# Gated linear attention and feed-forward block: block sums on VectorE, paired stores, an earlier load and later bias copies

## The chip, the cores and the metric

The kernel runs on one core of one Trainium2 chip. The metric is the time of one execution in microseconds (us); the time of a kernel is the median of its runs. Profiles come from one execution that the hardware profiler recorded, and their instants count from the first instruction of that execution.

## What is computed

```python
x  = A_x                                   # 1 x 2048 x 576, fp32
xn = layernorm(x)
q, k, v = split(xn @ wqkv)                 # 32 heads of 18
pq, pk = phi(q), phi(k)                    # phi(t) = (t + 1 if t > 0 else exp(t)) + 1e-6
kv = sum_s pk[s] (outer) v[s]              # no mask: one state per head for the whole sequence
z  = sum_s pk[s]
o  = (pq @ kv) / (pq . z + 1e-6)
s  = o @ wo
h  = gelu(xn @ w1 + b1)                    # 576 x 4608
g  = silu(h @ w2 + b2)                     # 4608 x 576
out = x + s * g
```

Everything is fp32. The kernel writes each operand of a matmul as a high part (a cast to the fp32r format of TensorE) and a low part (what the cast left), and multiplies high by high, high by low and low by high. The large products are also written as seven products of half-size blocks instead of eight, which is why sums and differences of blocks are needed as operands beside the blocks themselves.

## The kernel before

**Three phases.** Phase 1 (to about 152 us) normalises x, makes its operands, and computes keys, values and the state. Phase 2 (about 152 to 312 us) computes the queries and the attention output. Phase 3 (from about 312 us) is the feed-forward block with its gate. The rows of x are handled as eight pairs of row tiles in phases 1 and 2, and as two halves in phase 3.

**Rounds of phase 2.** The loop over `r` (line 1094 and after) has one round for a pair of tiles; `base = (NPAIR + r) * NSP`, with 14 steps to a round. In rounds 1 to 7 TensorE runs the seven products of `Proj` (steps 0 to 6, in the order 1, 6, 7, 5, 2, 4, 3; lines 382 to 408), which make the queries, and from round 2 two `Attend` (28 matmuls each, in steps 7 to 12), which multiply the weighted queries of two rounds earlier by the folded output weights. After each `Attend` come five transposes for the round before (`transpose_p`). Each product of `Proj` is emptied out of its PSUM bank by VectorE or ScalarE: product 6 at line 393, product 7 at line 396, products 5, 4 and 3 at line 386, the first half of a query at line 402. The bank of product 7 is used again by product 4, and that of product 5 by product 3, so these two wait for the emptying.

**The order is written out by hand.** `add(step, function)` puts a call on a list, and `at_step(step)` runs the list of that step behind the product of that step. All of phases 1 and 2 is inside `in_order()`, which fixes the order of every engine and of the DMA queue of SyncE (SP) to that of the program text: an instruction that waits holds everything behind it on its engine. In phase 3 the order of TensorE, VectorE, ScalarE and GpSimd is fixed in the same way; that of SP is not.

**Rest.** D is 576 = 4 x 128 + 64, so each half of the inner dimension is 2 x 128 + 32 rows. The last 32 rows of x and of w1 do not fill a pass of TensorE. `Rest` (line 912) therefore stacks the high part of four things of 32 rows with their low parts, so that one pass does all of their products. One `Rest` handles one such stack: seven of them are made, `RESTS` names them (two of x, five of w1), and the `Rest` number r is loaded in round r and worked on in round r + 1. Its steps are

- the load of 128 x 512 fp32 raw rows into a tile of the pool `stg` (line 917; six buffers, shared with the raw wo rows, the folded weights and the attention outputs),
- `hi(0)` on ScalarE and `lo(0)` on VectorE for three blocks, as they are (lines 923 and 927),
- `store(0)`: four DMAs on SP, one for each group of 32 rows, because the stack holds each of the two parts twice (line 934),
- `sums` on GpSimd: four subtractions or additions of 128 x 128 blocks, in place (lines 940 and 942),
- `hi(1)`, `lo(1)`, `store(1)` for the four sums.

`hi` takes a buffer of the pool `w1r` under the tag `stw`, of which there are two. From round 3 on, the sums of w2 blocks (`w2_hi`, `w2_lo`, lines 533 to 540) take the same two buffers, twice in a round, at steps 9 and 11, and give them back when their store has landed.

**The fold.** Round 0 multiplies the state into wo (`fold_wo`, line 847) and moves the result by three rows of SP copies (lines 858 and 861) into other partitions. `wo` is loaded ahead of it at line 816. The raw rows of the first `Rest` are loaded behind it, at step 9 of round 0.

**Phase 3** runs 18 blocks of 28 steps, nine to a half of the rows: 14 steps of `Up` (two groups of seven products of seven matmuls) and 14 of the products with w2, which add into `macc`. `macc` begins as a copy of the bias b2: `set_bias` (line 1254, ScalarE), four copies of 128 x 1152, at steps 2, 3, 5 and 6 of the first block of half 0 and at steps 12, 13, 15 and 17 of the first block of half 1. The bias itself is loaded, spread over all partitions, by `load_bias` (line 1247) into a buffer under the tag `w2t6`. The same buffer is taken next by `load_sum(7)` (line 1329, at step 5), into which `sum7` (line 520, a DMA of GpSimd's queue that adds, at step 16) adds another block. `W2_SUMS_FIRST` gives the steps at which three ready operands of w2 are loaded back in the first block.

Of the kernel before, what the change touches and what calls it, by code (L numbers as in the profile page):

```python
# [8 lines left out]
F32 = mybir.dt.float32  # L9
# [6 lines left out]
P = 128  # L16
# [10 lines left out]
RW = 32  # L27
# [11 lines left out]
NPAIR = NT // 2  # L39
# [6 lines left out]
def linear_attention_gated_ffn(ctx, tc, x, wqkv, wo, w1, w1e, b1, w2, b2, out):  # L46
    nc = tc.nc
# [77 lines left out]
    xe_dram = [dram.tile([P, 4, 7, P], F32, name=f"xe_dram{i}") for i in range(2)]  # L125
    we_dram = [dram.tile([P, 4, 7, P], F32, name=f"we_dram{i}") for i in range(NB4)]
# [19 lines left out]
    class Weight:  # L146
# [28 lines left out]
        def sums(self, raw, eng):  # L175
            r4 = raw.rearrange("p (k f d) -> p k f d", k=4, f=2)
            f0a, f0b, f1a, f1b = r4[:, 0:2, 0], r4[:, 2:4, 0], r4[:, 0:2, 1], r4[:, 2:4, 1]
            self.t = [
                stage_w1(f"wt{i}")[:, : 2 * D].rearrange("p (i k d) -> p i k d", i=2, k=2)
                for i in range(2)  # L180
            ]
            a, b = self.t
            T = {4: a[:, 0], 5: a[:, 1], 6: b[:, 0], 7: b[:, 1]}
            for i, u, v in ((5, f1a, f0a), (6, f1b, T[5]), (7, f1b, f1a), (4, f0b, T[6])):
                eng.tensor_tensor(T[i], u, v, op=SUB)
# [358 lines left out]
    def add(step, fn, *args):  # L544
        plans.setdefault(step, []).append((fn, args))
# [105 lines left out]
    def plan_pair(p):  # L651
# [19 lines left out]
        add(base + 3, do_state, p - 1)  # L671
        if p == 1:
            sums(1, (0, 0, 0, 1, 1), 1, 6, GP)
            add(base, phi_max, k_ts[0][1], e_t[1])
            add(base, phi_add, k_ts[0][1])
# [11 lines left out]
            add(base + 5, x_rest, 2, 1)  # L687
            add(base + 5, x_lo, 2, 1)
            sums(2, (6, 6, 6, 6, 7), 8, 9, GP)
            add(base + 5, x_lo_tmp, 2)  # L690
            add(base + 6, wkq.sums_hi, 1)
# [8 lines left out]
        else:  # L700
# [6 lines left out]
            if p + 1 < NPAIR:  # L707
                q = p + 1
                add(base, x_norm, q, 1)
                add(base + 3, transpose_x, q, 1)  # L710
                add(base + 3, x_hi, q, 1)
                add(base + 3, x_rest, q, 1)
                sums(q, (4, 4, 4, 6, 5), 7, 10, DV)
                add(base + 4, x_lo, q, 1)
                add(base + 6, x_lo_tmp, q)
# [39 lines left out]
    for p in range(1, NPAIR):  # L755
        plan_pair(p)
        base = p * NSP
# [22 lines left out]
    def q_tiles(r):  # L780
        return [r_bufs[(2 * r + s) % 4] for s in range(2)]
# [11 lines left out]
    base = NPAIR * NSP  # L793
# [118 lines left out]
    class Rest:  # L912
# [15 lines left out]

        def store(self, g):
            t, at = self.t, slice(3 * g, (3, 7)[g])  # L930
            for j in range(4):
                v = t[:, j % 2 if self.of_x else j // 2].bitcast(F32)
                dst = (xe_dram if self.of_x else we_dram)[self.i][RW * j : RW * (j + 1)]
                nc.sync.dma_start(dst.rearrange("r c i j -> (r c) i j")[:, at], v)

        def sums(self):
            a, b, c, d = (self.s[:, k] for k in range(4))
            tt = nc.gpsimd.tensor_tensor
            if self.of_x:
                tt(d, a, d, op=SUB), tt(c, c, d, op=SUB), tt(a, c, a, op=ADD), tt(b, b, c, op=SUB)  # L940
            else:
                tt(a, d, a, op=SUB), tt(d, c, d, op=SUB), tt(c, c, a, op=SUB), tt(b, b, c, op=SUB)
# [125 lines left out]
                    t, self.ops[i] = op_tile(w1p, [W1_K[i], P], tag, bufs, f"w{i}_{n}")  # L1068
                nc.sync.dma_start(t.bitcast(F32), w1_dram[n % NP, i])

    rests, kept = {}, []
    RESTS = ((0, True), (0, False), (1, False), (2, False), (3, False), (4, False), (1, True))
    X_OVER = {1: (xSH, 8, 0), 2: (xH, 7, 1), 4: (xH, 4, 2)}
    X_EXTRA = (5, 3, 6, 7)
# [15 lines left out]
    for r in range(NPAIR + 2):  # L1090
        base = (NPAIR + r) * NSP
# [3 lines left out]
        if r < NPAIR:  # L1095
            a, b = q_tiles(r)
# [15 lines left out]
        if 1 <= r < NPAIR:  # L1112
            a, b = q_tiles(r)
            at = base + 2 * (r == 2)
# [12 lines left out]
        if 3 <= r <= 7:  # L1127
            n = 2 * r + 3
            for j in range(2):
                add(base + (4, 5)[j], w2_sum, n + j, True)  # L1130
                add(base + (9, 11)[j], w2_hi, n + j)
                add(base + (10, 11)[j], w2_lo, n + j)
        if r < NPAIR - 1:
            i, of_x = RESTS[r]
            add(base + (1 if r else 9), lambda r=r, i=i, of_x=of_x: rests.update({r: Rest(i, of_x)}))
        if 1 <= r < NPAIR:
            at = base + (5 if r == 1 else 1)
            for g, k in ((0, 0), (1, 4)):
                add(at + k, lambda r=r, g=g: rests[r - 1].hi(g))
                add(at + k, lambda r=r, g=g: rests[r - 1].lo(g))  # L1140
                add(at + k + 2, lambda r=r, g=g: rests[r - 1].store(g))
            add(at + 2, lambda r=r: rests[r - 1].sums())
        if r == NPAIR - 1:
            add(base + 8, load_x_over, 0)
        if r == 0:
# [18 lines left out]
        if 1 <= r < NPAIR:  # L1164
            for s in range(2):
                at = Attend(r - 2, s) if r >= 2 else None
# [14 lines left out]
        elif r == NPAIR:  # L1181
            w = w1t[0]
            at = Attend(r - 2, 0)
# [6 lines left out]
            at = Attend(r - 2, 1)  # L1190
# [12 lines left out]
        elif r > NPAIR:  # L1203
            for s in range(2):
                at = Attend(r - 2, s)
# [27 lines left out]
    kept = None  # L1233
# [7 lines left out]
    C11, C12, C21, C22, U1 = range(5)  # L1241
# [341 lines left out]
    PW2 = {1: 3, 7: 4, 3: 6}  # L1583
    PW2_FIRST = {1: 3, 2: 4, 7: 8, 3: 9}
    W2_SUMS_NEXT = {5: 23, 6: 27}
    W2_SUMS_FIRST = {4: 4, 5: 6, 6: 10}
    W2_NEXT = {1: 15, 2: 17, 7: 19, 4: 21, 5: 23, 3: 25, 6: 27}
    PH = dict(
        S={(7, 0): 7, (5, 0): 8, (6, 0): 10, (3, 0): 11, (7, 1): 13, (5, 1): 14, (6, 1): 15, (3, 1): 15},
# [19 lines left out]
    for step in range(n_chunks):  # L1609
        half, c = divmod(step, NC)  # L1610
        base = step * NS
        plain = step == n_chunks - 1
        h = HOps(c)
        if c == 0:
            if half:
                add(base + 2, load_bias)
            for at, m in zip((12, 13, 15, 17) if half else (2, 3, 5, 6), (C11, C22, C21, C12)):
                add(base + at, set_bias, m)
        if half == 0:
            plan_w1(add, w1t[2 * step + 1], base, **P1)  # L1620
# [7 lines left out]
            if step == 0:  # L1628
                for i, at in W2_SUMS_FIRST.items():
                    add(at, w2t[0].load, i)  # L1630
# [79 lines left out]
        for j in range(CF // 2):  # L1710
            n = 2 * step + j
# [54 lines left out]
```

## Time and profile before

| | us |
|---|---|
| median of 3 runs | 1143.37 (1142.31 to 1144.32) |
| the profiled execution | 1141.5 |
| its span, first to last instruction | 1139.7 |
| TensorE / VectorE / ScalarE / GpSimd busy | 1102.4 / 808.2 / 515.4 / 464.4 |
| first query product of round 3 | at 200.17 |
| end of the rounds (the last two attention tiles begin) | at 294.86 |
| moved by DMA | 295.0 MB, 259 GB/s on average |

The span lies 1.8 us below the time of the same execution and 3.7 us below the median. Busy time of TensorE is modelled for overlapping matmuls, so it says when the engine had work, not that it worked at its peak. "PEclk" in the views is the granted clock of TensorE as a share of full speed, and "DMA share" is the mean busy share of the 16 DMA engines.

### The profile page before, as it was taken

The page shows a single profiled execution, that of the slowest core. Times are in us where ns is not written, and L with a number is a line of the kernel's source. Part 1 is how long each engine was busy: PE and PEld are TensorE (multiplying, and loading weights), DVE is VectorE, ACT ScalarE, POOL GpSimd, SP SyncE. Part 2 cuts the span into 40 slices and gives each one's busy share as a digit, 9 for nine tenths or more (in the row PEclk, how much of TensorE's full clock was granted, in tenths as well). Part 3 has the DMA queues.
Part 4 walks back from the last instruction along what each step waited for, and adds up shares of the span by engine and source line. Part 5 has one row for each costly group of instructions (what it writes and reads, how often), then busy time and mean ns, then how long its engine had stood idle before and what let it go on. Part 6 is the DMA issues. An engine that isn't in the chain of part 4 may idle for free.

```text
span 1139.7 us, 19018 instructions
## 1 busy us (share of the span) xinstructions
PE 1102.4 (97%) x6888; PEld 1015.4 (89%) x6888; DVE 808.2 (71%) x1260; ACT 515.4 (45%) x945; POOL 464.4 (41%) x445
## 2 busy tenths in 40 slices
PE   8999996888979999999999999999999999999998
PEld 8999996888969889899899898998998988989988
DVE  6777476657558888888888898684674764755776
ACT  7776454444454454444435445543242242342342
POOL 6853524554524525525445344133232242341310
PEclk9999998999989999999999999999999999999999
DMA  5987838997797887967968969998766667767343
GB/s 199 322 282 261 276 90 267 346 352 289 289 368 223 311 280 243 349 223 259 347 209 288 320 190 328 384 390 292 231 218 230 219 213 227 223 223 234 92 151 114
DMA packets 116219, 295.02 MB, mean 259 GB/s; under 512 B 12637, under 2 KB 31581, under 8 KB 114079
## 3 DMA queue, kind: packets, MB, share of 16 engines
q1 hardware_dynamic: 110655, 282.61, 70.4%
q0 software_dynamic: 4896, 10.03, 5.2%
q8 instruction: 54, 0.88, 0.3%
q10 hardware_dynamic: 576, 1.18, 0.3%
q14 instruction: 38, 0.31, 0.1%
HBM read 180.39 MB, written 108.66 MB: 254 GB/s over the span
## 4 chain that ended last, share of the span: by engine, by line
PE 81%; DVE 6%; DMA 5%; ACT 4%; issue 2%; POOL 1%; SPq 1%; ACTq 0%; POOLq 0%; DVEq 0%
PE pm L1413 33%; PE zy L1274 10%; PE e L1274 10%; PE a L1274 10%; PE b L1274 5%; PE pl L434 4%; PE pd L1528 2%; PE e L378 1%; DMA op<-w2o 1%; PE a L378 1%; PE ps_kva L487 1%; PE z L378 1%; DMA rs0True<-xr_dram 1%; DMA rs2False<-w1e 1%; DMA x<-x 1%
## 5 line engine op out<-in xcount | busy, mean ns | idle before, releaser
L993 ACT CAST h_h<-g 128x512 fp32r<-128x512 f32 x204 | 120.1, 621 | 137.5 <-PE pm L1413 136.4
L996 DVE TENSOR_TENSOR h_l<-g,h_h 128x512 fp32r<-128x512 f32 x204 | 160.7, 788 | 3.1 <-ACT h_h L993 3.1
L1421 DVE TENSOR_TENSOR macc<-macc,pm 128x576 f32<-128x576 f32 x136 | 102.2, 751 | 39.2 <-PE pm L1413 39.1
L1274 PE MATMUL a<-xH,wa 128*128 128x512 f32 x288 | 101.4, 393 | 0.0
L1423 DVE TENSOR_TENSOR macc<-pm,macc 128x576 f32<-128x576 f32 x98 | 74.2, 757 | 22.4 <-PE pm L1413 20.9
L1381 POOL TENSOR_TENSOR mid<-g 128x512 f32<-128x512 f32 x34 | 44.0, 1294 | 107.7 <-ACT g L1282 107.7
L1282 ACT ACTIVATE g<-b,b1c 128x512 f32<-128x512 f32 x36 | 24.8, 688 | 131.3 <-DVE b L1300 131.3
L1291 ACT COPY mid<-a 128x512 f32<-128x512 f32 x36 | 21.2, 588 | 98.4 <-PE a L1274 98.4
L1274 PEld LDWEIGHTS a<-xH,wa 128*128 128x128 f32 x288 | 54.2, 188 | 11.3
L1375 POOL TENSOR_TENSOR g<-g 128x512 f32<-128x512 f32 x34 | 50.6, 1488 | 25.6 <-DVE h_l L996 24.0
L1294 DVE TENSOR_TENSOR mid<-b,mid 128x512 f32<-128x512 f32 x36 | 24.7, 686 | 46.4 <-PE b L1274 41.2
L1274 PE MATMUL a<-xL,wa 128*128 128x512 f32 x144 | 56.2, 390 | 0.0
L1274 PE MATMUL e<-xSH,wb 128*128 128x512 f32 x144 | 51.5, 398 | 4.8 <-DVE b L1300 4.7
L1378 POOL TENSOR_TENSOR g<-g 128x512 f32<-128x512 f32 x34 | 51.1, 1503 | 11.3 <-DVE h_l L996 8.3
L1499 POOL TENSOR_TENSOR fin1l<-fin1h,fin1l 128x288 f32<-128x288 f32 x8 | 6.5, 807 | 119.0 <-DMA fin1l<-s_dram 61.1
L1274 PE MATMUL zy<-xH,w 128*128 128x512 f32 x144 | 51.8, 401 | 0.0
L1274 PE MATMUL zy<-xSH,w 128*128 128x512 f32 x144 | 50.9, 394 | 0.0
L1274 PE MATMUL b<-xSH,w 128*128 128x512 f32 x144 | 50.5, 391 | 0.0
L1274 PE MATMUL e<-xSH,w 128*128 128x512 f32 x144 | 50.4, 390 | 0.0
L1020 POOL TENSOR_TENSOR mid<-w1raw 128x256 f32<-128x256 f32 x17 | 13.2, 778 | 89.4 <-DMA w1raw<-w 45.1
L1372 POOL TENSOR_TENSOR g<-g 128x512 f32<-128x512 f32 x34 | 47.1, 1386 | 2.7
L996 DVE TENSOR_TENSOR h_l<-mid,h_h 128x512 fp32r<-128x512 f32 x34 | 42.0, 1234 | 5.8 <-ACT h_h L993 5.8
(965 smaller groups left out, 3680.1 us busy)
## 6 DMA issues: line engine op xcount, KB each, us to landing
op<-w SPq DMA_DIRECT2D x72, 256.0 KB
w<-op SPq DMA_DIRECT2D x72, 256.0 KB
we<-we_dram SPq DMA_DIRECT2D x36, 448.0 KB
w2raw<-w SPq DMA_DIRECT2D x10, 1152.0 KB
op<-w2o SPq DMA_DIRECT2D x19, 576.0 KB
w1raw<-w SPq DMA_DIRECT2D x18, 512.0 KB
op_a<-wa SPq DMA_DIRECT2D x18, 512.0 KB
wa<-op_a SPq DMA_DIRECT2D x18, 512.0 KB
```

What stands on the lines that cost most here:

```text
L378: nc.tensor.matmul(ps, st, mv, start=first and n == 0, stop=n == len(seq) - 1, skip_group_check=True,)
L434: nc.tensor.matmul(self.ps[n], st, self.wk(hl, k, n), start=(i == 0), stop=(i == n_all - 1))
L993: nc.scalar.copy(pair[0], src)
L996: eng.tensor_tensor(pair[1], src, pair[0].bitcast(F32), op=SUB)
L1274: nc.tensor.matmul(ps.rearrange("p (c j) -> p c j", c=4), st, mv, start=first and n == 0, stop=n == len(seq) - 1, skip_group_check=True,)
L1372: tt(src[5, pr], A(1, 1), A(1, 0), op=SUB)
L1375: tt(src[6, pr], src[5, pr], A(0, 0), op=ADD)
L1378: tt(src[3, pr], src[6, pr], A(0, 1), op=SUB)
L1381: tt(src[7, pr], A(0, 0), A(1, 0), op=SUB)
L1413: nc.tensor.matmul(ps[:, q, :HD], hs[p][st][:, cs], m[:, p, :], start=(n == 0 and i not in CHAIN), stop=(n == len(seq) - 1), skip_group_ch ...
L1421: nc.vector.tensor_tensor(dst, dst, src, op=SUB)
L1423: nc.vector.tensor_tensor(dst, src, dst, op=ADD)
```

## The change

1. `store` issues two DMAs instead of four. Each writes one part to both places that hold it; its source repeats the tile with a step of zero, behind the partitions.
2. `sums` runs on VectorE instead of GpSimd.
3. The first `Rest` is made ahead of the loop, behind the loads of wo and ahead of the fold, instead of at step 9 of round 0.
4. In rounds 2 to 7, `hi(0)` and `lo(0)` move from step 1 to step 2, `store(0)` from 3 to 4, `sums` from 3 to 2; `hi(1)`, `lo(1)` and `store(1)` keep their steps 5 and 7. In round 1, `hi(0)` and `lo(0)` keep step 5, `sums` moves from 7 to 5, `hi(1)` and `lo(1)` from 9 to 8 and `store(1)` from 11 to 10.
5. In the first block of half 0, `set_bias` moves to steps 12, 13, 15 and 17, as in half 1.
6. One load of a ready w2 operand in the first block moves from step 10 to step 18.

```diff
         def store(self, g):
             t, at = self.t, slice(3 * g, (3, 7)[g])
-            for j in range(4):
-                v = t[:, j % 2 if self.of_x else j // 2].bitcast(F32)
-                dst = (xe_dram if self.of_x else we_dram)[self.i][RW * j : RW * (j + 1)]
-                nc.sync.dma_start(dst.rearrange("r c i j -> (r c) i j")[:, at], v)
+            n = t.shape[2] * P
+            for j in range(2):
+                v = t[:, j].bitcast(F32).rearrange("p i j -> p (i j)")[:, None].to_broadcast([P, 2, n])
+                if self.of_x:
+                    dst = xe_dram[self.i].rearrange("(a b r) c i j -> b (r c) a (i j)", a=2, b=2)[j]
+                else:
+                    dst = we_dram[self.i].rearrange("(b a r) c i j -> b (r c) a (i j)", a=2, b=2)[j]
+                nc.sync.dma_start(dst[:, :, at.start * P : at.stop * P], v)
 
         def sums(self):
             a, b, c, d = (self.s[:, k] for k in range(4))
-            tt = nc.gpsimd.tensor_tensor
+            tt = nc.vector.tensor_tensor
...
-    rests, kept = {}, []
+    kept = []
+    rests = {0: Rest(0, True)}
...
-        if r < NPAIR - 1:
+        if 0 < r < NPAIR - 1:
             i, of_x = RESTS[r]
-            add(base + (1 if r else 9), lambda r=r, i=i, of_x=of_x: rests.update({r: Rest(i, of_x)}))
+            add(base + 1, lambda r=r, i=i, of_x=of_x: rests.update({r: Rest(i, of_x)}))
         if 1 <= r < NPAIR:
-            at = base + (5 if r == 1 else 1)
-            for g, k in ((0, 0), (1, 4)):
+            at = base + (5 if r == 1 else 2)
+            for g, k in ((0, 0), (1, 3)):
                 add(at + k, lambda r=r, g=g: rests[r - 1].hi(g))
                 add(at + k, lambda r=r, g=g: rests[r - 1].lo(g))
                 add(at + k + 2, lambda r=r, g=g: rests[r - 1].store(g))
-            add(at + 2, lambda r=r: rests[r - 1].sums())
+            add(at, lambda r=r: rests[r - 1].sums())
...
-    W2_SUMS_FIRST = {4: 4, 5: 6, 6: 10}
+    W2_SUMS_FIRST = {4: 4, 5: 6, 6: 18}
...
-            for at, m in zip((12, 13, 15, 17) if half else (2, 3, 5, 6), (C11, C22, C21, C12)):
+            for at, m in zip((12, 13, 15, 17), (C11, C22, C21, C12)):
                 add(base + at, set_bias, m)
```

## The prediction

> **What bounds the kernel now.** First the stretches of the run, to see where TensorE, the engine with the most work, is not working. Columns: stretch, its length, then busy us of TensorE (PE), its weight loads, VectorE (DVE), ScalarE (ACT), GpSimd (POOL), then granted clock, DMA share, GB/s.
>
> ```profile
> 165.00:200.00 35.00, 25.62 (x177) 24.57 (x176) 23.75 (x43) 15.11 (x32) 14.55 (x17) 0.90 0.77 240
> 200.00:300.00 100.00, 88.84 (x622) 85.92 (x621) 63.65 (x110) 45.21 (x96) 55.73 (x52) 0.95 0.86 312
> 300.00:370.00 70.00, 63.27 (x367) 56.27 (x366) 45.25 (x71) 35.10 (x67) 29.07 (x29) 0.95 0.91 311
> 370.00:1090.00 720.00, 719.95 (x4262) 653.41 (x4261) 526.18 (x742) 294.30 (x522) 272.49 (x239) 1.00 0.77 260
> ```
>
> From 370 to 1090 us TensorE idles 0.05 us, so nothing is to be had there, and the change touches nothing there but the bias copies at half 1, which stay. Between 165 and 370 us it idles 9.4 + 11.2 + 6.7 = 27.3 us, and its clock falls to 0.90 to 0.95. Every edit lies in this stretch. Next the timeline of TensorE there, for who ends the idle time (last bracket: idle us before it, and the releaser).
>
> ```profile
> 181.41 0.47 PE L898 MATMUL ptp<-ident,pbuf 128*128 128x128 f32 x1 [7.08 <-ACT pbuf L890]
> 223.91 0.40 PE L378 MATMUL z<-wkq_h,xH 128*128 128x288 f32 x1 [1.53 <-DVE scr L396]
> 325.53 0.80 PE L1274 MATMUL e<-xSH,wb 128*128 128x512 f32 x1 [3.63 <-DVE b L1300]
> ```
>
> These are three separate stalls: one early, one that comes back in each round, one in the first feed-forward block. The releasers are vector engines; what held those is in the chain of waits, here for one round (start, us, what).
>
> ```profile
> 222.26 0.52 ACT re2False L923
> ...
> 229.74 0.46 POOL rs2False L942
> ...
> 230.87 1.25 DVE re2False L927
> ...
> 234.03 0.58 ACT s L971 x2
> ...
> 236.44 0.68 ACT w2o L533
> ...
> 238.02 3.43 DMA op<-w2o
> 241.53 0.52 ACT re3False L923
> ```
>
> The chain closes on itself: hi(0) of a stack (line 923) waits for the landing of a w2 sum, whose buffer it takes; line 396 of VectorE, which TensorE awaits at 223.91, stands behind lo(0); hi(1) waits for the sums on GpSimd; VectorE waits in lo(1) (230.87) behind that, the queries behind lo(1), and the next w2 sum (236.44) behind those on ScalarE. It takes 241.53 - 222.26 = 19.3 us. What TensorE needs for a round follows from the chain where it carries it: a product of six matmuls, one of eight, the transposes, and 27 of an attention tile's 28 matmuls.
>
> ```profile
> 135.06 0.79 PE z L378 x6
> 135.85 1.07 PE e L378 x8
> 304.36 0.74 PE ptp L898 x5
> 305.10 3.61 PE ps_s L963 x27
> ```
>
> That is 3 x 0.79 + 4 x 1.07 + 2 x 0.74 + 2 x 3.74 = 15.6 us. So the chain sets the rounds, and TensorE loses 3.7 us in each.
>
> **Part 1: the first load ahead of the fold.**
>
> ```profile
> 143.16 2.67 SPq L816 DMA_DIRECT2D wo<-wo  x5
> 170.57 10.10 DMA rs0True<-xr_dram
> 171.51 0.46 SPq L917 DMA_DIRECT2D rs0False<-w1e  x1
> 180.70 0.51 ACT L923 CAST re0True<-rs0True 128x384 fp32r<-128x384 f32 x1 [8.17 <-DMA rs0True<-xr_dram]
> 190.54 0.40 PE L378 MATMUL e<-wkq_h,xSH 128*128 128x288 f32 x1
> 155.00:160.00 5.00, 5.00 (x37) 4.83 (x36) 1.98 (x7) 0.54 (x2) 0.00 (x0) 1.00 0.00 0
> L173 DVE TENSOR_TENSOR wkq_rl<-rr,wkq_rh x2: 746/1124/1503, 11.9 to 153.3; 128x576 fp32r<-128x576 f32 x2
> L934 SPq EVENT_SEMAPHORE  x28: 17/17/17, 178.1 to 289.2; - x28
> ```
>
> The load now comes on SP right behind the five of wo, which end at 145.8. Five of the six buffers of the pool then hold wo; the sixth was the raw rest rr, last read at 153.3 to 154. The DMA engines stand still then (share 0.00), so the load lands before 165, and ScalarE loses its 8.17 us of waiting. The folded rows each move one buffer on, to the wo block whose product they follow anyway, so that costs nothing. What is late next: hi(0) of the second stack, in round 2. Its raw rows (171.51) are still issued behind the reloads of x, two places behind the load that landed at 170.57 + 10.10 = 180.7, and SP's first wait at the stores ended only at 178.1, so that the buffer of the first store comes back no sooner. I estimate 182 to 184 us for data and buffer. Behind that stand hi(0) and lo(0) (1.1 together), the sums (1.2, below) and line 386 (0.4) ahead of product 3, which starts at 184 to 187 where it started at 190.54. From the middle, 185.5, I take off 0.8 for the low clock behind an idle stretch of some 4 us: **-4.2 us** (3 to 6.5). If the buffer of rr came free only behind the fold, it would be 0.
>
> **Part 2: the rounds.** Removed from the chain: 2.0 us of GpSimd sums, and with them the wait of hi(1). Added on VectorE: four operations of 128 x 128. No row shows one there; the nearest are
>
> ```profile
> 310.61 0.42 DVE L996 TENSOR_TENSOR w<-w1raw,w 128x256 fp32r<-128x256 f32 x1
> L909 DVE TENSOR_TENSOR tl<-ptp,th 128x512 fp32r<-128x512 f32 x9 | 6.2, 686 | 1.7 <-ACT th L905 1.7
> ```
>
> From 0.42 for 256 columns and 0.69 for 512, 128 columns come to 0.29 us, four to 1.2. The other end is lo(1) above, 1.25 us for 512 columns while GpSimd works: 1.8 times the price, 2.1 us for four. I take 1.2, since GpSimd no longer adds blocks there; below nothing it can't be, as these are instructions more on an engine of the chain. The Trainium skill ("GPSIMD Engine Reference", Specifications) says that GpSimd shares its SBUF interfaces with VectorE and contends with instructions of two SBUF inputs, which these are; by it alone the price is the 2.1, and a round 0.9 us longer.
>
> hi(0) now stands one product later, so line 396 and product 4 run ahead of it, and product 3 waits instead. From the landing, X: hi(0) 0.5, lo(0) 0.6, sums 1.2, line 386 0.4, so product 3 starts at X + 2.9; it takes 1.1 and the first attention tile 3.7, to X + 7.8. From the copies of that tile (234.03) to the w2 cast (236.44) ScalarE needs 2.4 as now, so the cast stands at X + 10.2, where it is now at X + 14.2 (236.44 - 222.26). From there to the next X it is 5.1 as now. The new round is 15.3 us, just under TensorE's own 15.6.
>
> But DMA moves the same bytes in less time.
>
> ```profile
> 220.00:240.00 20.00, 18.18 (x125) 17.50 (x123) 13.06 (x23) 8.51 (x18) 10.63 (x11) 0.91 0.98 350
> 205.00:210.00 5.00, 4.79 (x36) 4.57 (x35) 2.76 (x8) 0.70 (x2) 3.25 (x5) 1.00 1.03 424
> we_dram<-re2False SPq DMA_DIRECT2D x4, 256.0 KB
> we_dram<-re2False SPq DMA_DIRECT2D x4, 192.0 KB
> ```
>
> 350 GB/s over 19.3 us are 6.8 MB for a round; at the fastest rate shown, 424, they take 15.9 us, at the present one 19.3. I take 400, near the fastest, so 16.9 for the two or three rounds with the most loads; the others lie between TensorE's 15.6 and that, and 16.4 is my mean. The paired stores move the same 1.8 MB in the same runs of 1.5 and 2 KB; they save SP two issues a group, which lie beside its wait for lo(1), so I cost them at 0.
>
> ```profile
> 200.17 0.38 PE L378 MATMUL a<-wkq_h,xH 128*128 128x288 f32 x1
> 294.86 0.51 PE L963 MATMUL ps_s<-kw_h,th 128*128 128x288 f32 x2
> ```
>
> Rounds 3 to 7 take 94.7 us now. Five of 16.4 are 82: **-12.7 us** (-4 with rounds of 18.1, -16.7 with 15.6).
>
> **Part 3: the bias copies.**
>
> ```profile
> 322.95 1.15 ACT L1254 COPY macc<-b2b 128x1152 f32<-128x1152 f32 x1 [6.05 <-DMA b2b<-b]
> 328.89 2.92 PE zy L1274 x7
> 331.81 1.62 PE a L1274 x7
> 336.08 0.33 SPq L1329 DMA_DIRECT2D w2s<-w  x1
> 361.71 0.67 ACT L993 CAST w__4249<-w2s 128x576 fp32r<-128x576 f32 x1
> ```
>
> ScalarE waits 6.05 us for the bias, with the casts of the next weights behind it; VectorE and so TensorE wait for those (3.63 us at 325.53). After it two products of seven matmuls run at a low clock: 3.36 (325.53 to 328.89) and 2.92 where one takes 1.62. With the copies ten steps later the bias has landed long before. That is 3.6 + 1.7 + 1.3 = 6.6. Against it: four copies of 1.15 us, 4.6 us of ScalarE, fall into steps 12 to 17, some 8 us in which it also makes the operands of the products; I take 1 us for that. And the copies hold the buffer that load_sum(7) takes: now issued at 336.08, behind the last copy, it moves to behind step 17, five steps into the products, and the cast of its sum, at 361.71 now, has perhaps 1 us left. I take **-5.6 us** (0 to -6.6). The later load of the w2 operand has eight steps to its use: 0.
>
> **Sum.** -4.2 - 12.7 - 5.6 = -22.5. The profiled execution took 1141.5 us (span 1139.7); it becomes 1119. The median is 1.9 above it: 1143.4 - 22.5 = **1121 us**.
>
> **Rivals.**
> *DMA sets the rounds.* The DMA share in the rounds is 0.98 already. If 350 GB/s is what this mix of short runs gives, rounds stay near 18.5 and part 2 brings 2: 1143.4 - 4.2 - 2 - 5.6 = 1131.5. For it: share 0.98. Against it: 424 GB/s in a stretch of such a round.
> *The bias edit gives back what it takes.* If SP keeps load_sum(7) in the written place, it holds the loads behind it for twelve steps of 1.6 us, and the w2 block for the next step lands late; part 3 is 0: 1126.5. Against it: in half 1 the copies stand at these steps and TensorE idles 0.05 us.
> *TensorE's pace everywhere.* -6.5 - 16.7 - 6.6 = -29.8: 1113.5.
> *The early load isn't early* (the buffer is not free before the fold): part 1 is 0, 1125.5.
> *Slower: the paired store runs on few DMA engines.* If its two copies and not the 128 partitions decide how it is split, two of 16 engines carry 1.8 MB a round: 1/8 of 400 GB/s, 37 us a round against 19.3. Seven rounds of +17.5 and part 3 make some +117: 1260. It decides below four engines (18 us). For it: the fold's copies of about 120 rows, under 0.3 MB each, ended only at 178.1, in stretches at half share. Against it: the partitions stand first on both sides of the new store. The Trainium skill ("DMA: Bandwidth & Descriptors", Rules for kernel authors) says that a repeat of c copies put outermost confines a DMA to c engines; by that rule this store, with its repeat second, keeps all 16.
>
> **Chances.** Forecast 0.57 (its own range 1114 to 1128); DMA sets the rounds 0.16; bias edit gives back 0.10; TensorE's pace 0.07; load not early 0.04; slower 0.03; nothing moves for a reason not seen 0.03. Range **1111 to 1134**: it takes in both ends of part 2 and 2 us for the clock that rounds without idle time would win and leaves the slower case and no change out. A measurement of this kernel tells 0.2% (2.3 us) from no change. Faster 0.94, same 0.03, slower 0.03.
>
> **What would show it.** Right: the chain no longer names rs0True; hi(0) of the second stack is the next wait, near 183; line 396 stands ahead of lo(0) and TensorE waits, if at all, at product 3; hi(1) waits for no one; X to X is 15.7 to 17 with DMA at 380 GB/s or more; ScalarE has no idle ahead of line 1254, and the first feed-forward block shows no clock below 0.9. Wrong: rounds above 18 with the DMA share at 1; ScalarE or VectorE waiting for the w2 sum at 361; the w2 store landing in over 5 us.

## The result, and the profile after

| | before | changed |
|---|---|---|
| median, us | 1143.4 (1142.3 to 1144.3) | 1130.6 (1128.6 to 1132.0) |
| the profiled execution, us | 1141.5 | 1128.6 |
| its span, us | 1139.7 | 1126.9 |
| first query product of round 3 | 200.17 | 197.60 |
| end of the rounds (round 8 begins) | 294.86 | 289.62 |
| first product of the feed-forward block | 312.40 | 306.85 |
| first product with w2 | 344.29 | 330.67 |

The changed kernel takes 0.9887 of the time before, 95% interval 0.9869 to 0.9905: 12.8 us less, where 22.5 were forecast. Lines stand four or five further down in the changed kernel: 934 is now 938, 963 is 967, 993 is 997, 1254 is 1259 and 1274 is 1279, while 378 to 927 stay; the sums stand at 944 and 946.

First the same stretches as before, in the changed kernel (columns as in the prediction):

```profile
165.00:200.00 35.00, 27.66 (x196) 26.95 (x195) 24.27 (x52) 17.18 (x36) 11.98 (x10) 0.90 0.87 294
200.00:300.00 100.00, 88.40 (x642) 86.82 (x641) 79.79 (x134) 46.70 (x94) 49.73 (x32) 0.97 0.88 314
300.00:370.00 70.00, 68.47 (x382) 59.88 (x382) 51.59 (x79) 40.62 (x77) 29.81 (x30) 1.00 0.96 334
370.00:1090.00 720.00, 719.65 (x4259) 652.80 (x4258) 526.78 (x741) 292.55 (x517) 273.29 (x238) 1.00 0.76 256
```

The second row is the surprise. In the 100 us from 200 on, most of them rounds, TensorE works no more than before (88.4 and 88.8), and VectorE counts as busy for 79.8 us instead of 63.7, in part with waits inside its instructions, as shown below. TensorE's idle time from 300 to 370 is nearly gone, and the clock there is 1.00.

From the instants in the table the gain can be split: 2.6 us up to round 3, 2.7 in rounds 3 to 7 (92.0 instead of 94.7), 0.3 in the attention tiles behind them, 8.1 from the first feed-forward product to the first product with w2 (23.8 instead of 31.9). In the next 23 us 0.9 is lost. Together 12.8.

Now for whom TensorE waits in the rounds (the view of waits of the changed kernel, 195 to 290 us: us in total, times, longest):

```profile
PE e L378 <- DVE scr L386: 7.1, 3, 2.7
PE e L378 <- DVE rt L386: 4.5, 2, 2.2
```

That is one wait of 2.2 to 2.7 us in each round, at product 3 (e), for line 386, where VectorE empties the bank of product 5. Here is round 4 on VectorE and GpSimd (timeline: start, us, engine, line, operation), with product 3 itself:

```profile
220.12 0.46 DVE L396 TENSOR_TENSOR scr<-z,scr 128x288 f32<-128x288 f32 x1
220.50 0.74 DVE L874 TENSOR_REDUCE den<-e 128x32 f32<-128x576 f32 x1
...
221.49 0.35 DVE L878 RECIPROCAL den<-den 128x32 f32<-128x32 f32 x1
221.76 0.49 DVE L927 TENSOR_TENSOR re2False<-rs2False,re2False 128x384 fp32r<-128x384 f32 x1
222.29 2.11 DVE L946 TENSOR_TENSOR rs2False<-rs2False 128x128 f32<-128x128 f32 x4
224.31 0.45 DVE L386 SCALAR_TENSOR_TENSOR rt<-e,scr 128x288 f32<-128x288 f32 x1
...
221.99 1.28 POOL L881 TENSOR_TENSOR pbuf<-scr,den 128x576 f32<-128x576 f32 x1 [4.41 <-DVE den L878]
...
224.82 0.40 PE L378 MATMUL e<-wkq_h,xSH 128*128 128x288 f32 x1 [2.23 <-DVE rt L386]
```

VectorE has no gap from line 396 to line 386. Between them stand `den_sum` (220.50 to 221.8; the reduction, a small operation and the reciprocal), lo(0) and the four sums. The reciprocal releases `den_div` on GpSimd (line 881), and the sums begin 0.3 us after it. The four sums one by one (the view of that line: shortest, median and longest in ns, first and last start):

```profile
L946 DVE TENSOR_TENSOR rs0False<-rs0False x4: 291/292/293, 184.7 to 185.6; 128x128 f32<-128x128 f32 x4
L946 DVE TENSOR_TENSOR rs2False<-rs2False x4: 291/293/1131, 222.3 to 224.1; 128x128 f32<-128x128 f32 x4
```

In round 2, where GpSimd is idle, each takes 0.29 us. In round 4 one of the four, the first, takes 1.13 us and the others 0.29. That reads as a wait for GpSimd's instruction to end (221.99 + 1.28 = 223.27) and not as a slowdown; the experiments below test it.

### The profile page after: what moved, and what is told of

It is laid out like the page before. It is cut to its first block, busy times and chain, and to the rows that moved or that the text cites. A ratio compares the mean times of both kernels' runs of the same rounds, so it can differ in the third digit from the quotient of the medians.

```text
span 1126.9 us, 18961 instructions
## 1 busy us (share of the span) xinstructions
PE 1096.0 (97%) x6888; PEld 1011.6 (90%) x6888; DVE 822.2 (73%) x1288; ACT 517.4 (46%) x945; POOL 456.0 (40%) x417
## 4 chain that ended last, share of the span: by engine, by line
PE 69%; DMA 1%; DVE 1%; ACT 1%; issue 1%; DVEq 0%; ACTq 0%
PE pm L1418 34%; PE zy L1279 10%; PE a L1279 10%; PE e L1279 10%; PE b L1279 5%; PE pd L1533 2%; DMA op<-w 1%; DMA op_b<-wb 1%; DVE macc L1526 0%; ACT macc L1527 0%; DVE h_l L1000 0%; DVE b L1305 0%; ACT g L1287 0%; ACT L1287 0%; DVE xs L1477 0%
## 5 line engine op out<-in xcount | busy, mean ns | idle before, releaser
L1380 POOL TENSOR_TENSOR g<-g 128x512 f32<-128x512 f32 x34 | 50.6, 1490 | 24.1 <-DVE h_l L1000 22.5
```

The costliest lines, as they stand in the source:

```text
L1380: tt(src[6, pr], src[5, pr], A(0, 0), op=ADD)
```

## The experiments

Each time stands beside runs of the kernel before on the same chip. "Rounds" is the time from the first query product of round 3 to the first attention tile of round 8, in the profiled execution of each; before it is 94.7 us, in the changed kernel 92.0, and 91.5 in the profile of its second run.

**The parts of the change, one at a time.** The later bias copies and the later w2 load alone, on the kernel before:

```diff
-    W2_SUMS_FIRST = {4: 4, 5: 6, 6: 10}
+    W2_SUMS_FIRST = {4: 4, 5: 6, 6: 18}
...
-            for at, m in zip((12, 13, 15, 17) if half else (2, 3, 5, 6), (C11, C22, C21, C12)):
+            for at, m in zip((12, 13, 15, 17), (C11, C22, C21, C12)):
```

> The kernel before with the later bias copies and the later load of one w2 operand alone. The forecast put this part at -5.6 (0 to -6.6): 1137.8. By the two traces, from the first product of the feed-forward block to the first product with w2 it is 31.9 us before and 23.8 after, and 0.9 is lost in the next stretch: -7.2, so 1136.2, if the stretch owes this to the bias alone. If a part of it comes from the earlier parts of the change (loads that land earlier), it is 1137.5 to 1140.

1135.0 us, 0.9940 of before (0.9921 to 0.9959): -6.8 (4.7 to 9.0 by the interval). From the first feed-forward product (312.80) to the first with w2 (339.18) it is 26.4 us, 5.5 less than before. The other 2.6 us of that stretch in the changed kernel come with the other parts. So this part was worth what the forecast said, or about 1 more; the interval takes in both.

The first load alone, ahead of the fold:

```diff
-    rests, kept = {}, []
+    kept = []
+    rests = {0: Rest(0, True)}
...
-        if r < NPAIR - 1:
+        if 0 < r < NPAIR - 1:
             i, of_x = RESTS[r]
-            add(base + (1 if r else 9), lambda r=r, i=i, of_x=of_x: rests.update({r: Rest(i, of_x)}))
+            add(base + 1, lambda r=r, i=i, of_x=of_x: rests.update({r: Rest(i, of_x)}))
```

> The kernel before with the first load ahead of the fold alone (part 1). The forecast put it at -4.2. In the changed kernel product 3 of round 2 starts 4.1 us earlier (186.47 from 190.54), but round 3 starts only 2.6 us earlier (197.60 from 200.17), since the clock is low behind the wait at product 3. If that is all, 1141.9 becomes 1138.5 to 1139.5. If the rounds behind it, which are bound by their own chain, take the gain back (buffers and loads no earlier), it is 1141 to 1142.

1141.4 us, 0.9989 (0.9976 to 1.0001): -1.2, which can't be told from nothing. Round 3 starts at 198.73, 1.4 earlier, and the rounds, with their old order, take 97.0 us. The first reading failed and the second is near.

Part 2 alone (paired stores, sums on VectorE, the new steps), that is the changed kernel with the two parts above undone:

> The kernel before with part 2 alone (paired stores, sums on VectorE, the new steps), without the early load and the later bias copies. The forecast put part 2 at -12.7. By the stretch from round 3 to round 8 in the traces it is -2.7: 1139 to 1141. By what is left of 12.8 after the early load alone (-1.2) and the bias copies alone (-6.8) it is -4.8: 1137 to 1139. If the late load of the first stack delays the sums in rounds 1 and 2 on VectorE, whose queue holds more than GpSimd's, it is nothing or a loss: 1142 to 1144.

1140.5 us, 0.9977 (0.9967 to 0.9987): -2.6. The rounds take 92.0 us, as in the changed kernel, but round 3 starts 2.5 us later than in the kernel before (202.67): product 3 of round 2 starts 1.0 later (191.51), behind line 386 and the sums ahead of it on VectorE, and from there to round 3 it takes 1.5 more, as in the changed kernel. Alone the three parts make 6.8 + 1.2 + 2.6 = 10.6 us of the 12.8.

Four stores in a group again, in the changed kernel (the four lines marked with a minus in the diff of the change, in place of the eight with a plus):

> The changed kernel with four stores in a group again instead of two with a repeat. The forecast put this part at 0: 1130 to 1131.5. If four issues on SP held up the loads behind them, it is slower by 1 us or more; if the repeat makes a store slower to land, it is faster.

1132.2 us, 0.9914 (0.9895 to 0.9932), rounds 91.6. The changed kernel has 0.9887 and, run again, 0.9880, and its intervals touch this one: the pairing may be worth some 3 us or nothing. The rounds don't show it; from round 8 to the first feed-forward product this kernel takes 18.6 us, where the changed one took 17.2 and 17.8 in its two profiles.

The changed kernel once more, beside other runs:

> The changed kernel once more, beside the other runs of this chip: 1127 to 1132, sums of 1.1 to 1.3 us where GpSimd is idle (rounds 1 and 2) and of 2.1 in rounds 3 to 7.

1129.3 us, 0.9880 (0.9864 to 0.9896). The sums take 1.14 and 1.27 us in rounds 1 and 2 and 2.10 to 2.11 in rounds 3 to 7.

**The sums one step later.** Line 386 ahead of them:

```diff
-            add(at, lambda r=r: rests[r - 1].sums())
+            add(at + (r > 1), lambda r=r: rests[r - 1].sums())
```

> The changed kernel, with the sums of rounds 2 to 7 one step later, behind line 386 of product 5 and behind the second den_sum on VectorE. Theory A (VectorE's order): in the changed kernel TensorE waits 2.2 us at product 3 of every round because line 386 stands behind four sums that take 2.1 us. Then this wait goes, with it the low clock that follows it in rounds 3 and 5 (1.5 us each), and rounds 3 to 7 take 78 to 82 us instead of 92.0: 1117 to 1121 us in all, from 1130.6. Theory B (DMA sets the rounds): the wait at product 3 is only where the lateness shows; the rounds stay at 17.6 or more, with TensorE waiting elsewhere in them: 1129 to 1132.

1130.2 us, 0.9900 (0.9883 to 0.9916): no gain, rounds 92.5. Theory A's wait does fall (product 3 waits 0.7 us in two rounds and not at all in the others), but the time is lost elsewhere. Round 5 on VectorE and GpSimd:

```profile
241.24 0.44 DVE L386 SCALAR_TENSOR_TENSOR scr<-e,scr 128x288 f32<-128x288 f32 x1
...
242.86 4.48 DVE L946 TENSOR_TENSOR rs3False<-rs3False 128x128 f32<-128x128 f32 x4
247.26 0.45 DVE L386 SCALAR_TENSOR_TENSOR scr<-z,scr 128x288 f32<-128x288 f32 x1
...
241.05 1.29 POOL L881 TENSOR_TENSOR pbuf<-rt,den 128x576 f32<-128x576 f32 x1 [4.52 <-DVE den L878]
243.09 1.17 POOL L881 TENSOR_TENSOR pbuf<-rt,den 128x576 f32<-128x576 f32 x1 [0.74 <-DVE rs3False L946]
244.21 1.48 POOL L526 TENSOR_TENSOR w2r<-w2r 128x576 f32<-128x576 f32 x1
245.77 1.42 POOL L526 TENSOR_TENSOR w2r<-w2r,w2r 128x576 f32<-128x576 f32 x1
```

The same four sums now take 4.48 us. GpSimd has three instructions back to back, the second `den_div` and the two w2 additions, and the sums get through only in the gaps between them. The four one by one, in the view of their line:

```profile
L946 DVE TENSOR_TENSOR rs3False<-rs3False x4: 228/1341/1466, 242.9 to 245.9; 128x128 f32<-128x128 f32 x4
```

Three of the four take about 1.3 to 1.5 us. What stands behind the sums on VectorE is now late, and with it TensorE at the transposes, in the view of waits of this kernel:

```profile
PE ptp L898 <- DVE th L910: 8.9, 5, 2.0
```

That is 8.9 us in five rounds. Line 386 at 241.24 reads one operand from PSUM and runs inside GpSimd's instruction in its usual 0.44 us. The price is thus no factor on VectorE's time: an operation with two SBUF operands waits out the GpSimd instruction that it meets. The Trainium skill ("SBUF — State Buffer", section "SBUF: two separate sides") says that VectorE and GpSimd share a port pair by an exclusive lock, held for the whole instruction by whoever starts first. These rows agree with it.

**The sums back on GpSimd,** at the new step, behind the first `den_div`:

```diff
-            tt = nc.vector.tensor_tensor
+            tt = nc.gpsimd.tensor_tensor
```

> The changed kernel with the sums back on GpSimd, at the new step (2), behind den_div there. Theory A: VectorE has 2.1 us less ahead of line 386, product 3 starts some 2 us earlier in each round, rounds 3 to 7 take 79 to 84 us: 1118 to 1123. Theory B: no change, 1129 to 1132. Theory C (hi(1) is what counts, so that the engine of the sums matters less than their end): the sums end on GpSimd at about the time at which they end on VectorE now or up to 1 us later, and the rounds stay within 0.5 us of the present ones: 1129 to 1133.

1124.6 us, 0.9847 (0.9827 to 0.9867): about 5 us faster than the change as it stands, rounds 86.9. Theory A is right on the wait (product 3 waits 0.5 to 0.9 us in three rounds and not at all in two) and too low on the time (79 to 84 and 1118 to 1123). The next wait shows on ScalarE at the w2 cast (timeline of this kernel),

```profile
232.06 0.67 ACT L533 CAST w2o<-w2r 128x576 fp32r<-128x576 f32 x1 [1.89 <-DMA we_dram<-re2False]
```

which takes a buffer that a stack's store has not given back yet. The copies of the attention tiles stand behind it on ScalarE, and TensorE waits for those 4.4 us in three rounds.

**The sums on VectorE, but ahead of `den_sum`.** GpSimd is idle then:

```diff
             for s in range(2):
-                add(base + 2 + s + late, den_sum, r - 1, s)
-                add(base + 2 + s + late, den_div, r - 1, s)
+                n = base + (3 if 2 < r < NPAIR else 2 + s + late)
+                add(n, den_sum, r - 1, s)
+                add(n, den_div, r - 1, s)
```

> The changed kernel with both den_sum (and their den_div on GpSimd) at step 3 in rounds 3 to 7, so that lo(0), the four sums and line 386 stand ahead of them on VectorE, and GpSimd is idle while the sums run. Theory A2 (VectorE doesn't run an operation of two SBUF inputs while a GpSimd tensor_tensor runs, but waits out its rest, and what stands behind waits too): the sums take 1.1 to 1.2 us in rounds 3 to 7 instead of 2.1, line 386 ends near 2 us earlier, the wait of product 3 falls from 2.2 to 0.2 to 0.9 us, rounds 3 to 7 take 84 to 88 us instead of 92.0, 1122 to 1126 us in all. Theory B (DMA, or the landing of stores for the two buffers, sets the rounds): the sums are as short, but the rounds stay at 90 to 92, 1129 to 1131. Theory D (the sums cost 2.1 us of their own on VectorE): sums stay at 2.1 and product 3 waits 1.5 or more.

1128.8 us, 0.9880 (0.9860 to 0.9900): no gain, rounds 92.4. The sums take 1.27 us in rounds 3 to 6 and 1.14 in round 7, so theory A2 is right on their price and D falls. But in rounds 4 to 7 product 3 waits as long as before (2.0 to 2.6 us; 0.2 in round 3), since lo(0) now waits for hi(0) on ScalarE, and hi(0) for the landing of the w2 sum whose buffer it takes, 2.5 to 3.7 us in rounds 4 to 7 (timeline of this kernel, rounds 5 and 7):

```profile
238.37 0.56 DVE L927 TENSOR_TENSOR re3False<-rs3False,re3False 128x384 fp32r<-128x384 f32 x1 [1.52 <-ACT re3False L923]
238.96 1.27 DVE L946 TENSOR_TENSOR rs3False<-rs3False 128x128 f32<-128x128 f32 x4
...
276.93 0.51 ACT L923 CAST re1True<-rs1True 128x384 fp32r<-128x384 f32 x1 [3.70 <-DMA op<-w2o]
```

The profile names the store only in round 7; in rounds 4 and 5 it names an event that was over 0.6 and 1.0 us earlier, in round 6 none. That it is the buffer there too is shown by the run of this order with one buffer more, below, where hi(0) waits 0.5 us at most. Of theory B that half stands which names the two buffers. In the changed kernel hi(0) waits too (0.9 to 1.4 us in rounds 4 to 6), but VectorE is busy with line 396 and `den_sum` meanwhile, so nothing behind it shows the wait.

**A buffer of its own for the first w2 sum of a round,** so that the stacks and the second sum share the two. In the changed kernel alone:

```diff
-        pool, tag, bufs = (t1, "w2o", 1) if j == 8 else (w1r, "stw", 2)
+        pool, tag, bufs = (t1, "w2o", 1) if j == 8 else (w1r, "stw", 2) if j < 9 or j % 2 == 0 else (t2, "w2o2", 1)
```

> The changed kernel with the buffer of its own for the first w2 sum alone; sums on VectorE behind den_sum as they are. Theory F (two bounds lie side by side: VectorE's order, with sums of 2.1 us, and the two shared buffers): taking one away leaves the other, so product 3 still waits near 2 us for line 386 and rounds 3 to 7 take 89 to 92 us, 1127 to 1131 in all. Theory G (the buffers are the only bound, and the order on VectorE merely shows it): 83 to 86 us, 1121 to 1124.

1127.7 us, 0.9867 (0.9853 to 0.9881), rounds 89.7. Theory F: product 3 waits as in the changed kernel (the view of waits, 195 to 300 us),

```profile
PE e L378 <- DVE scr L386: 6.6, 3, 2.2
PE e L378 <- DVE rt L386: 4.5, 2, 2.2
```

hi(0) no longer waits here, and yet a round takes 17.5 to 17.7 us, as the rounds at full clock did in the changed kernel (17.6 to 17.7). Most of what the five rounds gain comes from the clock: one of them runs its first attention tile at a low clock and takes 1.5 us more, where in the changed kernel two do. Nothing in the runs ties that to the buffer.

With the buffer, and the sums on GpSimd:

> The changed kernel with the sums on GpSimd, as in the run of that name, and one more buffer: the first of the two w2 sums of a round takes a buffer of its own, so that the stacks and the second share the two they have. There ScalarE waited 1.4 to 1.9 us at each w2 cast for a store to land, and rounds 3 to 7 took 86.9 us, with a DMA share of 0.89 to 1.03. Theory E (the two buffers are the next bound): these waits go and rounds 3 to 7 take 79 to 82 us, 1117 to 1120 in all. Theory B2 (DMA's rate is the next bound): the DMA share stays at 0.98 or above at 350 to 385 GB/s, the wait moves to the loads (of raw w2, x or stacks), and rounds 3 to 7 take 85 to 87 us, 1123 to 1125.

1121.0 us, 0.9807 (0.9790 to 0.9823), rounds 83.1: between theories E and B2. The two heaviest rounds have a DMA share of 1.03, at 398 and 382 GB/s, and take 16.8 and 17.0 us.

With the buffer, and the sums on VectorE ahead of `den_sum`:

> The changed kernel with den_sum behind line 386, as in the run with the sums ahead, and the buffer of its own for the first w2 sum of a round; the sums stay on VectorE. If theories A2 and E hold together, rounds 3 to 7 take 78 to 82 us and the time is 1116 to 1120. If DMA's rate is next (B2), 85 to 87 us and 1123 to 1125. If the den_div that come later hold up the transposes behind the first attention tile, TensorE waits there and the gain is 2 us less.

1123.5 us, 0.9831 (0.9815 to 0.9848), rounds 84.5, by the numbers nearest to B2; that DMA's rate is what holds them is not shown. hi(0) waits 0.5 us at most, and in each round product 3 waits 0.2 to 0.7 and the transposes 0.5.

**Both, with the sums on GpSimd ahead of `den_div`:**

> The changed kernel with the sums on GpSimd, with den_sum and den_div behind line 386 and so behind the sums on GpSimd, and with the buffer of its own for the first w2 sum: the two steps that helped, put together in the other way. If line 386 behind den_sum was what was left at product 3 (0.5 to 0.7 us a round in the run with the sums on GpSimd and the own buffer), rounds 3 to 7 fall from 83.1 to 79 to 82 us and the time is 1117 to 1120. If the den_div, now 2 us later, hold up the transposes, or DMA's rate sets the two rounds with a share of 1.03, they stay at 83 to 86 us: 1120 to 1124.

1119.3 us, 0.9794 (0.9781 to 0.9808), rounds 81.3: the fastest, some 10 us below the change as it stands, by the first of the two readings. Nothing waits at product 3; what TensorE still waits for are the transposes (0.2 to 1.1 us in four rounds) and, once, a copy on ScalarE (0.9). Its five rounds (columns as above):

```profile
196.28:211.61 15.33, 15.33 (x119) 15.16 (x118) 11.64 (x20) 8.39 (x19) 11.88 (x12) 1.00 0.99 363
211.61:228.11 16.50, 15.37 (x119) 15.16 (x118) 12.29 (x21) 8.20 (x18) 9.36 (x10) 1.00 0.90 322
228.11:245.03 16.92, 15.65 (x120) 15.21 (x118) 12.67 (x22) 9.15 (x19) 11.99 (x12) 1.00 1.04 413
245.03:261.51 16.48, 15.41 (x119) 15.19 (x118) 12.81 (x21) 8.48 (x18) 9.35 (x10) 1.00 1.02 370
261.51:277.60 16.09, 15.75 (x120) 15.26 (x118) 13.53 (x22) 9.23 (x20) 12.46 (x12) 1.00 0.86 302
```

Side by side, rounds 3 to 7 in us:

| sums | two buffers | one more |
|---|---|---|
| VectorE, behind `den_sum` (the change) | 92.0, 91.5 | 89.7 |
| VectorE, ahead of it | 92.4 | 84.5 |
| GpSimd, `den_div` ahead | 86.9 | 83.1 |
| GpSimd, ahead of `den_div` | not tried | 81.3 |

## Why the prediction was right, and where it was not

**The sign and the range** were right; of 22.5 us 12.8 came. But 1130.6 lies outside the forecast's own range (1114 to 1128) and inside the stated one only because that was drawn wider, and it lies closest to a rival, "DMA sets the rounds" (1131.5). Part 2 fell 10.0 us short (2.7 instead of 12.7) and the time up to round 3 fell 1.6 short; the feed-forward block brought 1.6 more than its 5.6 (8.1 less the 0.9 behind it), and 0.3 came in between.

**Part 1** was right in its mechanism. The load is issued at 153.22 and lands 2.6 us later, hi(0) of the first stack no longer waits, and the next wait is the one named (timeline of the changed kernel):

```profile
183.52 0.51 ACT L923 CAST re0False<-rs0False 128x384 fp32r<-128x384 f32 x1 [3.30 <-DMA xe_dram<-re0True]
186.47 0.61 PE L378 MATMUL e<-wkq_h,xSH 128*128 128x288 f32 x1 [5.63 <-DVE rt L386]
```

and the clock behind it, in the view of stretches:

```profile
185.00:190.00 5.00, 3.53 (x15) 3.53 (x16) 4.82 (x11) 0.00 (x1) 0.81 (x1) 0.52 1.02 407
```

182 to 184 and 184 to 187 were forecast, 183.5 and 186.5 came, 1.0 later than the 185.5 that the sum used. Too small as well was the term for the low clock, 0.8: in the stretch with the end of the wait the granted clock was 0.52, and from product 3 to round 3 it took 11.1 us where it took 9.6, 1.5 more. So -2.6 came instead of -4.2, and that with the new order of round 2; the early load alone starts round 3 1.4 us earlier, and its -1.2 in the whole run can't be told from nothing.

**Part 2** failed at the step "From the landing, X: hi(0) 0.5, lo(0) 0.6, sums 1.2, line 386 0.4, so product 3 starts at X + 2.9" (the four terms make 2.7; where the other 0.2 comes from is not said), and a second time at "From there to the next X it is 5.1 as now". hi(0) in rounds 4 and 5 of the changed kernel, from its timeline:

```profile
219.81 0.51 ACT L923 CAST re2False<-rs2False 128x384 fp32r<-128x384 f32 x1 [0.94 <-DVE scr L393]
238.61 0.51 ACT L923 CAST re3False<-rs3False 128x384 fp32r<-128x384 f32 x1 [1.18 <-DVE th L910]
```

If 219.81 is taken as X, product 3, at 224.82, starts at X + 5.0. Three things were left out of the sum or priced too low:

- VectorE was not free at X. `den_sum` (1.3 us) stands at the same step, ahead of lo(0); I had moved hi(0) and lo(0) behind line 396 and not looked at what else is written at that step.
- The four sums took 2.1 us, not 1.2. The price of each, 0.29, was exact, and the other end of my range, 2.1, was the right one. But the reason that I gave for the low end, that GpSimd no longer adds blocks there, overlooked that `den_sum` releases `den_div` on GpSimd just ahead of the sums. The 1.8 as a factor was a chance hit: beside three GpSimd instructions the price is 4.5. The Trainium skill ("GPSIMD Engine Reference", Specifications) says that the two engines contend for such operations, and these rows agree; that the 2.1 worked out beside it met the row was luck, for it came from that factor.
- The next X came 13.8 us after product 3 (238.61) instead of 12.4. The first w2 cast of the round, whose buffer the next hi(0) takes, stands at X + 13.0 (232.83) instead of X + 10.2. From it to the next X it is 5.8 us instead of 5.1, since the sum's low part (line 538) takes 1.80 us on VectorE, where the second one takes 0.76. It meets `den_mul` on GpSimd (233.30 to 234.73). The second cast waits for a stack's store to give back its buffer, but the next hi(0) does not take that one (timelines of ScalarE and VectorE):

```profile
232.83 0.68 ACT L533 CAST w2o<-w2r 128x576 fp32r<-128x576 f32 x1 [0.19 <-DMA we_dram<-re2False]
235.26 0.67 ACT L533 CAST w2o<-w2r 128x576 fp32r<-128x576 f32 x1 [1.75 <-DMA we_dram<-re2False]
...
233.54 1.80 DVE L538 TENSOR_TENSOR w2o<-w2r,w2o 128x576 fp32r<-128x576 f32 x1 [0.80 <-ACT w2o L533]
235.97 0.76 DVE L538 TENSOR_TENSOR w2o<-w2r,w2o 128x576 fp32r<-128x576 f32 x1 [0.63 <-ACT w2o L533]
```

Besides, two of the five rounds ran at a lower clock: behind the stall at product 3 the attention tile took 5.2 us in rounds 3 and 5 (granted clock of these rounds 0.91) and 3.7 in rounds 4, 6 and 7 (1.00).

Of the signs named for part 2, product 3 as the place of the wait came. That a round takes 15.7 to 17 us with DMA at 380 GB/s or more did not (17.6 to 19.9 us at 252 to 360 GB/s), nor that hi(1) waits for no one (0.8 to 1.2 us in each round, for the sums or for a w2 store). One sign of being wrong did come: the one landing of a w2 store that the trace times took 6.4 us, where over 5 was named.

The table above shows that two bounds lie side by side, VectorE's order and the two shared buffers. Either alone holds the rounds at 90 to 92 us as long as the sums are on VectorE; with both gone they fall to 84.5, and to 81 to 83 with the sums on GpSimd. So the forecast's 82 us, and its figure for the heaviest rounds (16.9 at 400 GB/s), were met by the last kernel above, 81.3 with 16.9 and 16.5 at 413 and 370 GB/s, but not by the kernel that was forecast. That DMA's rate sets these rounds is not shown: in them TensorE waits for VectorE and ScalarE, and the runs leave open how far those wait for transfers.

**Part 3** was right, perhaps with somewhat more: 6.8 alone (4.7 to 9.0). Its first feed-forward block has no low clock and no wait for the bias, as forecast. For the copies among the products 1 us was taken off; 0.9 is lost in the stretch where they now stand. The wait for the w2 sum that I named as a sign against it did come, with no loss: by its row ScalarE waits 4.55 us, and TensorE works 20.0 of 20 us between 350 and 370 (timeline of ScalarE in the changed kernel).

```profile
353.60 0.67 ACT L997 CAST w__4221<-w2s 128x576 fp32r<-128x576 f32 x1 [4.55 <-DMA w2s<-w2s]
```

**The rivals.** "DMA sets the rounds" gave 18.5 us a round and 1131.5, and 18.4 and 1130.6 came; yet its mechanism is not what holds them, so it came close by chance. The same bytes went through in 81.3 us, at up to 413 GB/s, and the changed kernel's rounds have a DMA share of 0.72 to 0.99. "The paired store runs on few engines" fell: with four stores the rounds take 91.6 us, with two 92.0 and 91.5. The rule of the Trainium skill on repeats ("DMA: Bandwidth & Descriptors", Rules for kernel authors) agrees: with the repeat second the rounds reach a DMA share of 0.99. "The early load isn't early" (whose own terms make 1125.1, not 1125.5) and "the bias edit gives back" fell, and so did "TensorE's pace everywhere", with no round of the changed kernel under 17.6 us.

## What to carry to other kernels

Before an operation is put on another engine, list everything that is written at that step on its queue, in order, and what each entry wakes elsewhere: a `den_sum` ahead of the sums both stood in their way and started the GpSimd instruction that they then waited out. Where a loop of waits is cut, look for the loop beside it before summing; here an order on VectorE and two shared buffers each held the same round, and with the sums on VectorE only removing both paid. Work on VectorE with two SBUF operands was priced by the GpSimd instruction that it met, not by a factor, and the slower engine with room can be the better place.

## What the runs showed of the hardware

In these runs a VectorE operation with two SBUF operands that meets a running GpSimd tensor_tensor waits for its end: a sum takes 0.29 us alone, 1.13 when it meets the rest of one, about 1.3 to 1.5 when it meets a whole one, and four of them between 1.14 and 4.5 us. It goes beyond the sums. In round 5 of the changed kernel the second of two equal operations of line 468 meets a w2 addition (247.61 to 249.58), and it takes as long in the four other rounds:

```profile
247.53 0.76 DVE L468 SCALAR_TENSOR_TENSOR scr<-e,scr 128x576 f32<-128x576 f32 x1 [0.90 <-ACT e L465]
248.20 1.99 DVE L468 SCALAR_TENSOR_TENSOR scr<-scr 128x576 f32<-128x576 f32 x1
...
247.61 1.97 POOL L526 TENSOR_TENSOR w2r<-w2r,w2r 128x576 f32<-128x576 f32 x1
```

GpSimd seems to wait in the same way: this addition starts 0.1 us behind the first operation of line 468 and takes 1.97 us, where the same one took 1.42 with the sums one step later.

The clock after equal stalls differed: behind 2.23 us at product 3 the attention tile took 5.24 us in round 3 and 3.72 in round 4. The runs do not show what decides it.
